# A list-ordered attention and feed-forward kernel: other attention blocks, weights decoded in place, a gate kept in PSUM

## The chip, the cores and the metric

The kernel runs on one core of one Trainium2 chip. The metric is device time in microseconds, the median of the runs, lower is better. Before the change three runs took 772.35, 773.11 and 777.2 us.

## What is computed

Three layers on 4 sequences of 576 positions with 512 channels. q and k are drawn six times wider than v; the weights reach the kernel as float64.

```python
# 1. attention, 8 heads of 64; two results are added
q_d, k_d, v_d = means over 4 neighbouring positions      # 144 positions
out_d = softmax(q_d k_d^T / 8) v_d, each row repeated 4 times
out_local = softmax over |i - j| < 4 of (q k^T / 8), times v
x = out_d + out_local                                    # (4, 576, 512)
# 2. gated feed-forward, 512 -> 1024 -> 512
h = relu(x @ w_in)
c = conv_w[0]*h[s-1] + conv_w[1]*h[s] + conv_w[2]*h[s+1] # per channel
x = (h * sigmoid(c)) @ w_out
# 3. mixer: U is 576 x 32, V is 32 x 576, inner width 2048
u = x + (x^T @ U @ V)^T
out = u + relu(u @ w_ch1) @ w_ch2
```

## The kernel before

**Order.** Tiles come from pools, but no scheduler orders them: a string of some 2,600 words is read word by word, and each word emits a few instructions. So the order on each engine (PE the matrix engine, DVE the vector engine, ACT the scalar engine, POOL, and SP, which issues all DMAs) is the order of the list, and an instruction whose input is not ready holds all behind it on its engine.

**Attention** goes by 16 pairs of heads. q and k land as rows of positions (L315) and are transposed on PE, twelve transposes of 96 columns a pair (`transposes`, L408), then copied out of PSUM (`emit_qc`, `emit_kc`) and summed by fours (`emit_qsum` L439, `emit_ksum` L470). The band of the local part is cut into 10 blocks of 58 queries against 64 keys: a mask product of 320 columns per head (L511), then 20 small float32 products of 64 columns (L517), each with 64 rows of contraction; the trace has two records for each float32 product. The maximum is taken per block and head (L524); exp is one ACT instruction for each block and head, with its row sum as a by-product (L531, ten a pair); `emit_norm` multiplies by reciprocals. P is transposed in five pieces (L599), and 20 products of 58 columns make the local output (L635). The pooled part has three products of 144 columns (L553), six transposes (L604) and four products (L646). For the first eight pairs v is summed by fours on PE, as 20 products with a band matrix (`emit_Vp`, L492); for the other eight on POOL (L480). `emit_x` adds the two outputs in pieces, and `prep_x` splits x into a high and a low part with the columns next to the block's edge.

**Weights.** 16 tiles of 128x512 for layer 2 and 32 for layer 3 arrive as float64, 512 KB each. `decode` turns one into float32 in four steps, one on ACT (L217) and three on DVE (L219, L221, L224); `split_hi` (L229) and `split_lo` (L233) make the two parts.

**The products.** A product of two split operands is three passes. Tokens go in 6 blocks of 384. Layer 2 has 48 units (block and 128 inner channels): `g1` is 12 products of 386 columns (L882), `g2` is 9 of 512 (L944). Between them `relu1` (L893) copies from PSUM to SBUF, `conv_first` (ACT, L912), `conv_rest` (two on DVE, L918), `tanh` (ACT, L922), `gate` (DVE, L927), `gate_hi` (ACT, L932) and `gate_lo` (L935; 20 on POOL, 28 on DVE) follow, all in SBUF, so that the product's bank is free after `relu1`. Layer 3 has 96 units: `g3` (L1051) and `g4` (L1070), with `relu3` between. The mixer's rank-32 products stand between the layers.

**Space.** PSUM has eight banks. During attention four go to attention (`ps0`) and four to layer 2: three sums and one `g`. Before the layer-2 products start, the second four hold q and k transposes.

Of the kernel before, what the change touches and what calls it, by code (L numbers as in the profile page):

```python
# [169 lines left out]
def mixer_kernel(ctx, tc, q, k, v, w_in, conv_w, w_out, mU, mV, w_ch1, w_ch2, out, stop=9, dbg=None, early_end=False):  # L170

    nc = tc.nc
    B, H, S, D = q.shape
    P = 128
# [973 lines left out]
```

## Time and profile before

| | |
|---|---|
| runs | 772.35, 773.11, 777.2 us |
| span of the profiled execution | 771.8 us, 0.2% under the median; the page gives no other time for it |
| PE busy | 750.2 us, 97% |
| DVE busy | 427.6 us, 55%, nearly all in the first 430 us |
| ACT busy | 339.4 us, 44% |
| POOL busy | 158.2 us, 20% |
| moved by DMA | 48.7 MB in 81,203 packets, 61,916 of them under 512 B |

Busy time is the union of an engine's instructions. The matrix engine's records overlap, so that the distance from one start to the next, not the length of one record, is what an instruction costs there.

### The profile page before, as it was taken

The numbers are of one execution on the slowest core, as the hardware profiler recorded it, in microseconds if no ns is written. First come the engines' busy times: TensorE is split into PE (matmuls) and PEld (weight loads), VectorE is DVE, ScalarE is ACT, GpSimd is POOL, SyncE is SP. The second block draws the span as 40 slices with busy tenths as digits, with TensorE's granted clock in tenths as the row PEclk, the third lists the DMA queues.
The fourth block names the chain that finished last, engine by engine and source line by source line (L and its number), as shares of the span: only waits on it lengthen the run. The fifth ranks groups of instructions, "written<-read, shape, count | busy, mean of one in ns | idle before, by whom it ended". The sixth has DMA issues, their size and how long they took to land.

```text
span 771.8 us, 13685 instructions
## 1 busy us (share of the span) xinstructions
PE 750.2 (97%) x5382; PEld 669.8 (87%) x5382; DVE 427.6 (55%) x843; ACT 339.4 (44%) x1025; POOL 158.2 (20%) x233
## 2 busy tenths in 40 slices
PE   4889999999999999999999999999999999999998
PEld 3678888898888998888989889999999899989996
DVE  7888988988897888887888312212121221122111
ACT  3888878777676677675344112111111211111110
POOL 4355257343353111117510000000000000000000
PEclk9999999999999999999999999999999999999999
DMA  9867545343233111211244100100010000001001
GB/s 193 191 158 162 115 123 89 80 79 83 85 103 90 55 55 55 82 55 55 82 137 137 41 1 1 42 1 0 1 42 1 0 26 17 1 1 41 1 1 41
DMA packets 81203, 48.71 MB, mean 63 GB/s; under 512 B 61916, under 2 KB 74484, under 8 KB 81140
## 3 DMA queue, kind: packets, MB, share of 16 engines
q1 hardware_dynamic: 81140, 47.85, 24.0%
q8 instruction: 42, 0.69, 0.4%
q14 instruction: 21, 0.17, 0.1%
HBM read 43.11 MB, written 4.72 MB: 62 GB/s over the span
## 4 chain that ended last, share of the span: by engine, by line
PE 88%; DVE 4%; ACT 3%; DMA 2%; issue 1%; SPq 1%; POOL 0%; DVEq 0%; POOLq 0%; ACTq 0%
PE acc L1070 26%; PE g L1051 13%; PE gb L1051 13%; PE acc L944 11%; PE g L882 10%; PE O L635 3%; PE gb L882 2%; PE tr L408 1%; PE Sd L553 1%; PE O L646 1%; DMA w1t<-in_moe_w_in_dram 1%; PE vp L492 1%; PE S L517 1%; PE T L599 1%; DVE hc L918 1%
## 5 line engine op out<-in xcount | busy, mean ns | idle before, releaser
L1070 PE MATMUL acc<-w,a 128*128 128x512 f32 x864 | 216.5, 394 | 0.1
L1070 PEld LDWEIGHTS acc<-w,a 128*128 128x128 f32 x864 | 160.9, 188 | 29.9 <-ACT a L1059 0.4
L1051 PE MATMUL gb<-uT,w 128*128 128x384 f32 x576 | 111.8, 338 | 0.0
L1051 PE MATMUL g<-uT,w 128*128 128x384 f32 x576 | 111.7, 339 | 0.0
L944 PE MATMUL acc<-w,ghl 128*128 128x512 f32 x432 | 111.5, 396 | 0.1
L1051 PEld LDWEIGHTS gb<-uT,w 128*128 128x128 f32 x576 | 101.7, 188 | 3.8
L1051 PEld LDWEIGHTS g<-uT,w 128*128 128x128 f32 x576 | 101.6, 188 | 3.6
L1060 DVE SCALAR_TENSOR_TENSOR a<-gb,a 128x384 fp32r<-128x384 f32 x48 | 26.7, 557 | 125.1 <-ACT a L1059 125.1
L1060 DVE SCALAR_TENSOR_TENSOR a<-g,a 128x384 fp32r<-128x384 f32 x48 | 26.7, 557 | 123.5 <-ACT a L1059 123.4
L882 PE MATMUL g<-xhl,w 128*128 128x386 f32 (+1 forms) x456 | 93.0, 344 | 0.0
L944 PEld LDWEIGHTS acc<-w,ghl 128*128 128x128 f32 x432 | 79.6, 188 | 14.2 <-POOL ghl L935 0.5
L1059 ACT ACTIVATE a<-g 128x384 fp32r<-128x384 f32 x48 | 23.5, 490 | 141.8 <-PE g L1051 139.7
L882 PEld LDWEIGHTS g<-xhl,w 128*128 128x128 f32 x456 | 80.3, 189 | 4.1 <-issue 0.6
L1059 ACT ACTIVATE a<-gb 128x384 fp32r<-128x384 f32 x48 | 23.5, 489 | 125.1 <-PE gb L1051 119.9
L918 DVE SCALAR_TENSOR_TENSOR hc<-hc,cw 128x384 f32<-128x384 f32 x96 | 64.2, 673 | 9.7 <-ACT hc L912 7.7
L531 ACT ACTIVATE P<-S,nm 122x64 f32<-122x64 f32 x160 | 48.2, 319 | 7.0 <-DVE nm L524 6.0
L935 POOL TENSOR_TENSOR ghl<-hc,ghl 128x384 fp32r<-128x384 f32 x20 | 23.1, 1154 | 84.5 <-ACT ghl L932 84.4
L922 ACT ACTIVATE hc<-hc 128x384 f32<-128x384 f32 x48 | 25.1, 524 | 22.5 <-DVE hc L918 22.5
L531 ACT ACTIVATION_READ_ACCUMULATOR P<-S,nm 122x1 f32 x160 | 33.9, 212 | 0.0
L1039 DVE TENSOR_TENSOR uT<-ut,uT 128x384 fp32r<-128x384 f32 x24 | 13.3, 556 | 32.3 <-ACT uT L1038 32.1
L912 ACT ACTIVATE hc<-hc,cw 128x384 f32<-128x384 f32 x48 | 29.6, 617 | 1.0
L927 DVE SCALAR_TENSOR_TENSOR hc<-hc 128x384 f32<-128x384 f32 x48 | 28.3, 598 | 2.9 <-ACT hc L922 2.6
(139 smaller groups left out, 1016.8 us busy)
## 6 DMA issues: line engine op xcount, KB each, us to landing
wraw<-in_moe_w_ch_dram SPq DMA_DIRECT2D x29, 512.0 KB, 3.6
kr<-in_k_dram SPq DMA_DIRECT2D x32, 144.0 KB, 4.3
qr<-in_q_dram SPq DMA_DIRECT2D x32, 144.0 KB, 4.9
out_dram<-u SPq DMA_DIRECT2D x17, 256.0 KB, 2.1
w1t<-in_moe_w_in_dram SPq DMA_DIRECT2D x8, 512.0 KB, 4.4
w1t<-in_moe_w_out_dram SPq DMA_DIRECT2D x8, 512.0 KB, 4.8
vw<-in_v_dram SPq DMA_DIRECT2D x32, 128.0 KB, 3.8
vr<-in_v_dram SPq DMA_DIRECT2D x8, 288.0 KB
```

The source lines that it names most:

```text
L531: nc.scalar.activation(out=e["P"][:, i, h], in_=e["S", h][:122, i], func=AF.Exp, bias=e["nm"][:, h, i:i + 1], accum_out=e["sm"][:, i, h:h ...
L635: nc.tensor.matmul(O[rows, c:c + QB], e["vw"][rows, 2 * i + a], PT[rows, i, 64 * a:64 * a + QB], start=True, stop=True)
L882: nc.tensor.matmul(p[:, :wd], w[:, a, cc], xhl[g, cc][:, b, :wd], start=k == 0, stop=k == 3 * NCC - 1)
L912: nc.scalar.activation(out=flat(g, c), in_=inner(g, hts[n], 0), func=AF.Copy, scale=cw[:, f:f + 1])
L918: nc.vector.scalar_tensor_tensor(out=o, in0=inner(g, hts[n], k), scalar=cw[:, k * NF + f:k * NF + f + 1], in1=o, op0=ALU.mult, op1=ALU.add)
L922: nc.scalar.activation(out=cts[n], in_=cts[n], func=AF.Tanh)
L927: nc.vector.scalar_tensor_tensor(out=o, in0=o, scalar=1.0, in1=inner(g, hts.pop(n), 1), op0=ALU.add, op1=ALU.mult)
L944: nc.tensor.matmul(acc[g][c], t[:, a, c * P:(c + 1) * P], w[:, b], start=f == 0 and i == 0, stop=f == NF - 1 and i == 2)
L1051: nc.tensor.matmul(p[:, :TB], w[:, a, cc], uT[g, cc][:, b, :TB], start=k == 0, stop=k == 3 * NCC - 1)
L1059: nc.scalar.activation(out=t[:, 0], in_=p[:, :TB], func=AF.Relu)
L1060: nc.vector.scalar_tensor_tensor(out=t[:, 1], in0=p[:, :TB], scalar=0.0, in1=t[:, 0].bitcast(F32), op0=ALU.max, op1=ALU.subtract)
L1070: nc.tensor.matmul(acc2[g][c], t[:, a, c * P:(c + 1) * P], w[:, b], start=f == 0 and i == 0, stop=f == NF2 - 1 and i == 2)
```

## The change

All of the kernel around the two large layers is written anew, and the list with it (2,671 words).

The host lays data out anew, ahead of the timed program: q and k with channels on partitions, v cut into 32-row windows (each row stored more than once) and into groups of four, weights, U and V in the order of their tiles, the identity and the mask as data.

Attention has 24 blocks of 24 queries against 32 keys: per pair two mask products of 192 columns, 48 score products of 32 columns (64 rows of contraction, 24 result rows), softmax by one max, one subtract, one exp and one sum over all 12 groups of a row, three transposes of 128 columns, and 48 products of 24 columns (32 rows of contraction, 64 result rows). q and k are not transposed on PE any more, and v is summed by fours on POOL or DVE for all pairs. PSUM has two slots for attention work while layer 2 runs (`a0`, two banks; `b0`, one), and two banks `g` instead of one.

The convolution, tanh and gate of layer 2 write into the product's own PSUM bank; the gate moves the result to SBUF. All 48 `gate_lo` are on POOL. The raw float64 words land in the tile's final place, are decoded into one of three passing buffers, and the high part is written over the raw words. Three products of zeros (`sp`) stand at the start.

The list's counts up to the first layer-2 product: six pairs scored, four finished, 12.9 MB of loads issued (9 of qk, 576 KB each; 6 of vr, 288 KB; 7 of vw, 384 KB; 6 weights). The same up to the last decode of a weight: all of layer 2 and 15 units of layer 3, as before.

```diff
-        r = p0.tile([96, 6, 2, D], F32, name=f"{nm}r", tag=f"{nm}r", bufs=2)
-        for h in range(2):
-            nc.sync.dma_start(r[:, :, h], src[b, 2 * cc + h].rearrange("(c p) d -> p c d", p=96))
+        t = (xu if p % 3 == 2 else pa).tile([P, 2, S], F32, name="qk", tag=("qk0", "qk1", "xu3")[p % 3])
+        nc.sync.dma_start(t, qk[p])
...
+    def scores(p, n):
+        s = e["S"] = slot_a(n, "S")
+        for h in range(2):
+            nc.tensor.matmul(s[:, h, :6 * NW], identR, mask.rearrange("p j x -> p (j x)"), start=True, stop=False)
+        for k in range(6):
+            t, jh = divmod(k, 2)
+            for a in range(4):
+                i = 4 * (3 * jh + t) + a
+                for h in range(2):
+                    rows = slice(D * h, D * h + D)
+                    nc.tensor.matmul(s[32 * a:32 * a + NQ, h, NW * k:NW * k + NW],
+                                     e["qk"][rows, 0, NQ * i:NQ * i + NQ], e["qk"][rows, 1, WS[i]:WS[i] + NW],
+                                     start=False, stop=k == 5)
...
-        for i in range(5) if part is None else (part,):
-            nc.scalar.activation(out=e["P"][:, i, h], in_=e["S", h][:122, i], func=AF.Exp,
-                                 bias=e["nm"][:, h, i:i + 1], accum_out=e["sm"][:, i, h:h + 1])
+    def shifted(p):       # one subtract of the maxima, S -> P, 384 columns
+        nc.vector.tensor_tensor(...)
+    def exps(p):
+        nc.scalar.activation(out=t, in_=t, func=AF.Exp, scale=SCALE)
+    def rowsums(p):
+        nc.vector.tensor_reduce(out=e["sm"][:, :12], in_=..., op=ALU.add, axis=AX.X)
...
+    def pv_local(p, n):
+        for t in range(3):
+            for a in range(4):
+                for s in range(4):
+                    h, jh = divmod(s, 2)
+                    c = NQ * (4 * t + a)
+                    nc.tensor.matmul(o[D * h:D * h + D, jh, c:c + NQ], e["vw"][32 * s:32 * s + 32, t, a],
+                                     e["PT"][32 * s:32 * s + 32, t, 32 * a:32 * a + NQ], start=True, stop=True)
...
     def conv_first(n):
-        c = cts[n] = hc.pop(n)[:, 1, :TB]
+        c = cts[n] = gp.pop(n)[:, :TB]
...
+    def gate(n, move):
+        if move:
+            cts[n] = ph.tile([P, TB], F32, name="ct", tag="ct", bufs=2)
...
     def gtile():
-        gt[0] += 1
-        if "psb" in pools and gt[0] % 2:
-            return pools["psb"].tile([P, 512], F32, name="gb", tag="gb")
-        return pools["psg"].tile([P, 512], F32, name="g", tag="g")
+        return pools["psg"].tile([P, 512], F32, name="g", tag="g", bufs=2)
```

## Rows read from the trace of the kernel before

**Rows 1.** The page: busy time by engine, and the chain that ended last.

```profile
PE 750.2 (97%) x5382; PEld 669.8 (87%) x5382; DVE 427.6 (55%) x843; ACT 339.4 (44%) x1025; POOL 158.2 (20%) x233
PE 88%; DVE 4%; ACT 3%; DMA 2%; issue 1%; SPq 1%; POOL 0%; DVEq 0%; POOLq 0%; ACTq 0%
```

**Rows 2.** Windows: start and end, length, then each engine's busy time, clock, DMA share, GB/s.

```profile
0.00:20.00 20.00, 9.25 (x78) 7.85 (x79) 14.24 (x29) 8.39 (x27) 9.48 (x38) 1.00 0.98 194
20.00:80.00 60.00, 53.06 (x852) 45.44 (x850) 51.40 (x118) 50.96 (x225) 27.42 (x40) 0.97 0.74 164
80.00:200.00 120.00, 119.93 (x1310) 106.87 (x1310) 105.28 (x238) 93.54 (x348) 54.12 (x79) 1.00 0.43 95
...
380.00:400.00 20.00, 20.00 (x108) 18.21 (x107) 16.80 (x28) 9.54 (x19) 2.57 (x2) 1.00 0.49 148
430.00:772.00 342.00, 338.04 (x1714) 305.04 (x1712) 63.63 (x114) 46.64 (x95) 0.00 (x0) 1.00 0.04 14
```

**Rows 3.** The chain from 60 to 90 us: start, length, engine, tile, line.

```profile
64.20 0.91 PE Sd L553 x6
65.10 0.65 PE O L646 x8
65.75 1.31 PE O L635 x40
...
67.46 1.10 PE g L882 x6
...
70.27 0.32 PE T L599 x3
...
73.55 0.52 PE S L511 x2
74.07 0.72 PE S L517 x40
74.78 1.45 PE vp L492 x40
...
85.77 0.65 PE tr L408 x6
```

**Rows 4.** PE's timeline from 560 us: start, length of the run of records.

```profile
562.35 2.27 PE L1051 MATMUL gb<-uT,w 128*128 128x384 f32 x12
564.46 2.27 PE L1070 MATMUL acc<-w,a 128*128 128x512 f32 x9
566.56 2.27 PE L1051 MATMUL g<-uT,w 128*128 128x384 f32 x12
```

**Rows 5.** DVE's groups by line: busy us, mean ns, idle before.

```profile
L918 DVE SCALAR_TENSOR_TENSOR hc<-hc,cw 128x384 f32<-128x384 f32 x96 | 64.2, 673 | 9.7 <-ACT hc L912 7.7
...
L1060 DVE SCALAR_TENSOR_TENSOR a<-g,a 128x384 fp32r<-128x384 f32 x48 | 26.7, 557 | 123.5 <-ACT a L1059 123.4
...
L935 DVE TENSOR_TENSOR ghl<-hc,ghl 128x384 fp32r<-128x384 f32 x28 | 18.0, 644 | 5.2 <-ACT ghl L932 5.0
L524 DVE TENSOR_REDUCE nm<-S 122x5 f32<-122x320 f32 x32 | 14.9, 481 | 5.1 <-PE S L517 4.8
...
L221 DVE SCALAR_TENSOR_TENSOR wval<-wraw,wval 128x512 uint32<-128x512 uint32 x16 | 12.8, 798 | 0.5
...
L563 DVE TENSOR_REDUCE nmd<-Sd 96x3 f32<-96x432 f32 x16 | 9.5, 595 | 2.1 <-PE Sd L553 2.0
```

**Rows 6.** ACT's groups by line, the same columns.

```profile
L531 ACT ACTIVATE P<-S,nm 122x64 f32<-122x64 f32 x160 | 48.2, 319 | 7.0 <-DVE nm L524 6.0 <-PE vp L492 0.9
L531 ACT ACTIVATION_READ_ACCUMULATOR P<-S,nm 122x1 f32 x160 | 33.9, 212 | 0.0
L912 ACT ACTIVATE hc<-hc,cw 128x384 f32<-128x384 f32 x48 | 29.6, 617 | 1.0
L922 ACT ACTIVATE hc<-hc 128x384 f32<-128x384 f32 x48 | 25.1, 524 | 22.5 <-DVE hc L918 22.5
...
L893 ACT ACTIVATE hc<-g 128x386 f32<-128x386 f32 (+1 forms) x38 | 18.8, 494 | 9.6 <-PE g L882 7.1 <-DVE ghl L935 2.3
```

More of the change, by code (lines that the diff above doesn't have):

```diff
@@ L198, in mixer_kernel @@
[L198 to L213 removed]
+    xu = ctx.enter_context(tc.tile_pool(name="xu", bufs=1, reuse_waits="tile"))
@@ new lines, in clear, with spin_fill, spin, slot_a @@
+    def clear():
+        nc.gpsimd.memset(eps, 1e-9)
+        for t in qds:
+            nc.gpsimd.memset(t, 0.0)
+    def spin_fill():
+        t = pools["spin"] = xu.tile([P, 512], F32, name="spin", tag="xu0")
+        nc.vector.memset(t, 0.0)
+    def spin(n):
+        t = pools["spin"]
+        nc.tensor.matmul(slot_b(n, "spin"), t[:, :P], t, start=True, stop=True)
+    st = {}
+    for p in range(NPAIR):
+        st[p] = {}
+    def slot_a(n, name):
+        return (ps0 if n < 1 else pst).tile([P, 2, 512], F32, name=name, tag=f"a{n}")
@@ new lines, in stats, with view, maxima @@
+    def stats(e):
+        if "sm" not in e:
+            e["nm"] = pa.tile([P, 15], F32, name="nm", tag="nm", bufs=3)
+            e["sm"] = pa.tile([P, 15], F32, name="sm", tag="sm", bufs=3)
+    def view(s):
+        return s[:, :, :6 * NW].rearrange("p h (j x) -> p h j x", j=6)
+    def maxima(p):
+        e = st[p]
+        stats(e)
+        nc.vector.tensor_reduce(out=e["nm"][:, :12].rearrange("p (h j) -> p h j", h=2), in_=view(e["S"]),
+                                op=ALU.max, axis=AX.X, negate=True)
@@ new lines, in scores_d, with maxima_d, exps_d @@
+    def scores_d(p, n):
+        e = st[p]
+        t = slot_b(n, "Sd")
+        s = e["Sd"] = t[:96, :3 * SD].rearrange("p (j x) -> p j x", j=3)
+        for j in range(3):
+            nc.tensor.matmul(s[:, j], e["qd"][:, j], e["ss"][:, 1], start=True, stop=True)
+    def maxima_d(p):
+        e = st[p]
+        stats(e)
+        nc.vector.tensor_reduce(out=e["nm"][:96, 12:], in_=e["Sd"], op=ALU.max, axis=AX.X, negate=True)
+    def exps_d(p):
+        e = st[p]
+        t = e["Pd"] = pa.tile([96, 3, SD], F32, name="Pd", tag="Pd", bufs=2)
+        s = e.pop("Sd")
+        for j in range(3):
+            nc.scalar.activation(out=t[:, j], in_=s[:, j], func=AF.Exp,
+                                 bias=e["nm"][:96, 12 + j:13 + j], accum_out=e["sm"][:96, 12 + j:13 + j])
@@ new lines, in pv_pooled, with copy_od @@
+    def pv_pooled(p):
+        e = st[p]
+        pt = e["PTd"].rearrange("p c (j r) -> p c j r", j=3)
+        for h in range(2):
+            for c in range(2):
+                nc.tensor.matmul(e["O"][D * h:D * h + D, 0, 288:288 + SD].rearrange("p (j r) -> p j r", j=3),
+                                 e["vd"][:, h, c], pt[:, c, :, 48 * h:48 * h + 48], start=c == 0, stop=c == 1)
+    def copy_od(p, eng):
+        e = st[p]
+        t = e["xd"] = pa.tile([P, SD], F32, name="xd", tag="xd", bufs=2)
+        src = e["O"][:, 0, 288:288 + SD]
+        if eng == "ACT":
+            nc.scalar.activation(out=t, in_=src, func=AF.Copy, scale=0.25)
+        else:
+            nc.vector.tensor_scalar(out=t, in0=src, scalar1=0.25, scalar2=None, op0=ALU.mult)
@@ L350, in mixer_kernel @@
-    W1, W2 = {}, {}
-    N1, N2 = 2 * NF, 2 * NF2
-    raws, vals, steps = {}, {}, {}
-    def w_decode(k, make):
-        if k not in steps:
-            vals[k] = make()
-            steps[k] = decode(vals[k], raws[k])
-        next(steps[k], None)
-    pairs = iter(CFG.get("TR", ""))
-    def whole_tile(p, nm):
-        e = st.setdefault(p, {})
-        if nm + "t" not in e:
-            n = next(pairs, "")
-            e[nm + "t"] = pst.tile([P, 2, 512], F32, name="tr", tag="tr" + n, bufs=1 if n else 2)
-        return e[nm + "t"]
@@ L389, in spin @@
-    def spin(bank):
-        nc.tensor.matmul(bank[:, :5 * W], identR, mask, start=True, stop=True)
-    def transposes(p, nm, half=None):
-        if not 0 <= p < NPAIR:
-            return
-        e = st[p]
-        if half is None:
-            t = whole_tile(p, nm)
-            view = [t[:, a, :288] for a in range(2)]
-            e[nm + "ps"] = [(slice(0, S), t[:, :, :288])]
-        else:
-            t = bank([P, 512], "tr")
-            view = {half: t[:, :288]}
-            e[nm + "ps"] = [(slice(288 * half, 288 * half + 288), t[:, :288])]
-        for c in range(6):
-            if half is None or c // 3 == half:
-                nc.tensor.transpose(view[c // 3][:, (c % 3) * 96:(c % 3 + 1) * 96],
-                                    e[nm + "r"][:, c].rearrange("p h d -> p (h d)"), ident[:96, :96])
@@ L619, in half_tile @@
-    def half_tile(e, i):
-        e.setdefault("O", {})
-        if i not in e["O"]:
-            e["O"][i] = bank([P, 512], "O")
-        return e["O"][i]
-    def emit_PV(p, half):
-        if not 0 <= p < NPAIR:
-            return
-        e = st[p]
-        O = half_tile(e, half)
-        for i in (range(0, 4), range(4, 5))[half]:
-            for a in range(2):
-                c = 2 * QB * (i % 4) + QB * a
-                for h in range(2):
-                    rows = slice(64 * h, 64 * h + 64)
-                    nc.tensor.matmul(O[rows, c:c + QB], e["vw"][rows, 2 * i + a], PT[rows, i, 64 * a:64 * a + QB],
-                                     start=True, stop=True)
@@ new lines, in w_dec, with w_hi, w_lo @@
+    def w_dec(*k):
+        *k, step = k
+        k = tuple(k)
+        if step == 0:
+            vals[k] = pv.tile([P, 512], F32, name="wval", tag="wval")
+        dec(raws[k], vals[k], step)
+    def w_hi(*k):
+        pool, tag = w_home(k)
+        W[k] = pool.tile([P, 2, 512], F32R, name="w", tag=tag)
+        nc.scalar.activation(out=W[k][:, 0], in_=vals[k], func=AF.Copy)
+    def w_lo(eng, *k):
+        eng.tensor_tensor(W[k][:, 1], vals.pop(k), W[k][:, 0].bitcast(F32), op=ALU.subtract)
@@ L779, in conv_weights @@
-    def conv_weights():
-        for _ in decode(cval, craw):
-            pass
-        cps = bank([P, 512], "cps")
-        nc.tensor.transpose(cps[:, :NK * NF], cval, ident[:NK * NF, :NK * NF])
-        nc.vector.tensor_copy(cw, cps[:, :NK * NF])
-    pools = {}
-    def open_products():
-        pst.release()
-        pools["psg"] = ctx.enter_context(tc.tile_pool(name="psg", bufs=1, space=PSUM, side="right", reuse_waits="tile"))
-    NSA, NSB = CFG["NSA"], CFG["NSB"]
-    RANK = mU.shape[1]
@@ new lines, in px_hi, with px_lo, g1 @@
+    def px_hi(g, cc):
+        t = xhl[g, cc] = xt.tile([P, 2, XW], F32R, name="xhl", tag="xt")
+        nc.scalar.activation(out=t[:, 0, :runs(g)[1]], in_=px_src(g, cc), func=AF.Copy)
+    def px_lo(g, cc, eng):
+        wd = runs(g)[1]
+        t = xhl[g, cc]
+        eng.tensor_tensor(t[:, 1, :wd], px_src(g, cc), t[:, 0, :wd].bitcast(F32), op=ALU.subtract)
+    hts, cts, ghl, acc, U_, hps, Ht, gp, x2 = {}, {}, {}, {}, {}, {}, {}, {}, {}
+    def g1(n, cc):
+        g, f = divmod(n, NF)
+        wd = runs(g)[1]
+        if cc == 0:
+            gp[n] = gtile()
+        w = W[1, 2 * f].rearrange("p a (c j) -> p a c j", c=NCC)
+        for i, (a, b) in enumerate(((0, 0), (0, 1), (1, 0))):
+            nc.tensor.matmul(gp[n][:, :wd], w[:, a, cc], xhl[g, cc][:, b, :wd],
+                             start=cc == 0 and i == 0, stop=cc == NCC - 1 and i == 2)
@@ L987, in mix_out, with mix_h @@
+    def mix_h(b, part):
+        lo = slice(RANK, 2 * RANK)
+        if part == 0:
+            Ht[b] = pools["pm"].tile([P, DM], F32R, name="Ht", tag="Ht", bufs=2)
+            nc.scalar.activation(out=Ht[b], in_=hps[b], func=AF.Copy)
+        else:
+            nc.vector.tensor_tensor(Ht[b][lo], hps[b][lo], Ht[b][lo].bitcast(F32), op=ALU.subtract)
+    mx = {}
     def mix_out(pair, j):
-        p = pools["psb"].tile([P, DM], F32, name="mx", tag="mx", bufs=2)
+        p = mx[pair, j] = pools["psb"].tile([P, DM], F32, name="mx", tag="mx", bufs=2)
@@ L1056, in relu3, with ut_hi, ut_lo, g3 @@
-    def relu3(m):
-        p = gp.pop(("3", m))
+    def ut_hi(g, cc):
+        t = uT[g, cc] = xt.tile([P, 2, XW], F32R, name="uT", tag="xt")
+        nc.scalar.activation(out=t[:, 0, :TB], in_=ut[g, cc][:, :TB], func=AF.Copy)
+    def ut_lo(g, cc):
+        t = uT[g, cc]
+        nc.vector.tensor_tensor(t[:, 1, :TB], ut.pop((g, cc))[:, :TB], t[:, 0, :TB].bitcast(F32), op=ALU.subtract)
+    def g3(m, cc):
+        g, f = divmod(m, NF2)
+        if cc == 0:
+            gp["3", m] = gtile()
+        w = W[2, 2 * f].rearrange("p a (c j) -> p a c j", c=NCC)
+        for i, (a, b) in enumerate(((0, 0), (0, 1), (1, 0))):
+            nc.tensor.matmul(gp["3", m][:, :TB], w[:, a, cc], uT[g, cc][:, b, :TB],
+                             start=cc == 0 and i == 0, stop=cc == NCC - 1 and i == 2)
```

966 lines of the change are left out of this document (325 added, 641 removed), and 303 rows, old and new, of the table SEQ.

## The prediction

> **What bounds the kernel now.** I read the page's busy line and its chain first: PE is busy 97% of the span and makes 88% of the chain that ended last [rows 1]. So only what shortens PE's own work, or the time in which PE waits, can move the end. Where it waits is read from the windows [rows 2]: 10.75 us in the first 20, 6.94 in the next 60, nearly nothing from 80 to 430, and 3.96 behind 430, mostly the last block's way out; 21.7 us in all. DVE is the second engine to watch: 71%, 86% and 88% busy in the first three windows, and 366 of its 427.6 us lie ahead of 430 us [rows 1, 2]. ACT reaches 85% only from 20 to 80 us. DMA is nearly full in the first 20 us (share 0.98 at 194 GB/s); the weights' later loads moved 148 GB/s at a share of 0.49, so wider rows cost less per byte [rows 2]. Then I read prices from the chain, where each piece is what it put on the path [rows 3], and the pace of the large products [rows 4]: 12 records of 384 columns every 2.11 us and 9 of 512 every 2.10 us, 4.21 us a unit. 144 units make 606 us. None of them is changed: same records, same columns. The change acts on the other 165 us.
>
> **PE work that goes.** Per pair of heads: two sets of q and k transposes, 2 x 0.65 us; two of five P transposes, 2 x 0.107 (three took 0.32); the mask's columns fall from 640 to 384, so 0.52 becomes 0.31 if it goes by columns and stays 0.52 if by records; I take columns, since 320 columns are nearer to the product records than to the small ones [rows 3]. Together 1.72 us, times 16 = 27.5. The band products leave eight pairs, 8 x 1.45 = 11.6 [rows 3]. Removed: 39.1 us. Pooled scores, their transposes and products stay, piece for piece.
>
> **The small products** are the open price. Scores and local output are 20 float32 products each, 40 records, 0.72 + 1.31 = 2.03 us a pair; they become 48 each, 192 records. No row has a product of 32 or 24 columns. Records come every 18 ns for scores and 33 ns for outputs [rows 3]. The scores walk over four places of the array (two heads by two row halves), the outputs over two, and 4 x 18 and 2 x 33 are about the same: one place takes some 66 to 72 ns for 58 to 64 columns. If only that counted, the new scores (half the columns, eight places) would come every 4.5 ns and the new outputs (24 columns, four places) every 6.8, 1.1 us a pair. At the score row's 18 ns per record it is 3.5 us, at the output row's 33 ns it is 6.3. I take 10.5 ns, 2.0 us, as before: the nearest row is the score row, whose places are doubled and columns halved here, but part of its 18 ns may be a floor. So this term is 0, with ends of -15 and +69 us over 16 pairs before anything absorbs it.
>
> A rule speaks against this edit. The Trainium skill, "TensorEngine Tiling (Array Packing)", section Instruction Overhead, says that a matmul costs about 60 cycles however few its columns are and that one should not tile along a side that is already small. By that figure, 25 ns at 2.4 GHz, the two groups would be 4.8 us a pair, 44 us more over the kernel. The score row's 18 ns is already under it, so I don't take it as a floor; the mechanism is a rival below, priced from rows.
>
> **Start.** The first layer-2 product came at 67.5 us [rows 3]. In the new list six pairs are scored and four finished before it. DVE's share: six sums over 1152 columns at 1.35 us (480 ns for 320 columns and 595 for 432 give 1.03 ns a column), six times max, subtract and sum over 384 (0.55 each) and the pooled max (0.60), ten reciprocals at about 0.2, four adds of 576 columns (0.75), eight decode steps (about 0.7) [rows 5], 34 us with small ones. Loads issued ahead are 12.9 MB: 43 us at the later rate (148/0.49 = 302 GB/s), 65 us at today's early rate (194/0.98 = 198) [rows 2]; not all of them are needed by then, and the rows are now 3 to 4.6 KB. So DVE sets it: first data at about 6 us, 34 us of work with gaps, first product at 46 us (40 to 55). PE has done 27 us of work by then: 19 us idle, in the place of 17.7.
>
> **DVE next.** After the start the list is dense in DVE work. Up to the eighth pair's scores DVE has 131 us (the 34 above, then 97 of the same prices, with decode at 2.0 a tile, 0.67 for each low part on DVE, and 1.7 for each gate chain), PE 118. From 80 to 200 us DVE was 88% busy while PE, not DVE, was the limit [rows 2]; as the limit itself I take 94%. 6 + 131/0.94 = 145 us, so PE has 27 us idle by then instead of 19. At 88% it would be 37, at 100% 19. From there on PE has more work than DVE (84 against 57 us, then 87 against 72, 73 against 68), and PE is full again.
>
> **Gate in PSUM.** The two convolution steps cost 673 ns in SBUF; a like instruction with a PSUM operand costs 557 [rows 5], so DVE loses up to 11 us; ACT's 617 and 524 ns may become its 494 from PSUM [rows 6]. I cost this at nothing on the path beyond the DVE sums above. What it adds is a wait: the bank is held from `relu1` to the gate, 0.49 + 0.60 + 2 x 0.56 + 0.52 + 0.56 = 3.3 us in six steps between two engines, about 4 to 5 with crossings. Two banks g and a unit of 4.2 us leave PE, by the list, 3.8 to 8 us of other work until it needs the bank again, in many units about 5. I put 3 us on that (0 to 15): it is hidden except in the tightest units, and behind the waiting PE everything waits.
>
> **The rest.** ACT loses 82 us of exps and accumulator reads for some 9 us of single exps (16 of an estimated 0.55) [rows 6]: worth nothing on the path, as PE covers ACT; without that cover it is the same sign. `gate_lo` wholly on POOL takes 18 us off DVE [rows 5]; 28 more on POOL, even at 2 us each, leave its 158 us [rows 1] far under the span. Decode keeps its four steps. The three starting products lie in a wait for data. SP issues fewer, larger transfers; an early one that waits for a buffer holds those behind it, which I keep in the 40 to 55 above. The end is unchanged, 4 us idle.
>
> **The sum.** 771.8 span - 39.1 PE work + idle of (27 + 3 + 4) - 21.7 = 12.3 gives 745.0. The profiled execution shows only its span, 1.3 us below the median of the runs; with that, **746 us**.
>
> **Rivals.** *Record pitch.* If a small record costs what it cost in the output row, 33 ns, attention grows by (6.3 - 2.0) x 16 = 69 us; the eleven early pairs lie where PE waits for DVE, which absorbs up to 27: 746 + 42 = 788, slower. It decides from about 28 ns, where 4.4 us a pair would be lost to 3.4. For it: more records on smaller work. Against: the score row has 18. Chance 0.09. At 18 ns the same sum gives 746 + 23, less what is absorbed, 757 to 769: 0.11, half of it within 1%.
>
> *The bank wait.* If each of the six steps queues behind a decode step or an attention step of 0.6 to 0.8 us, the chain is 7 to 8 us and PE loses 1 to 2 us in some 40 units: 786 to 826. Against: the list interleaves the units, and most gaps exceed 5. Chance 0.06 for that; a mild form (8 to 15 us more, 754 to 761), with DVE at 88% or a start at 55 beside it, 0.22.
>
> *It comes out better:* 4 to 7 ns per record, a start at 40, DVE full, 705 to 727: 0.10. That the diff doesn't do what it says can hardly be: the transposes are gone from the program. My forecast's own case, 728 to 753, keeps 0.42.
>
> **Chances.** A measurement tells about 1% from no change, so faster is under 765.4. Faster: 0.42 + 0.10 + 0.22 + half of 0.11 = 0.80. Same: the other half and some of the bank wait and pitch rivals' lower ends, 0.10. Slower: 0.10. The range 720 to 770 leaves out the heavy rivals (0.15 or a little less) and the lowest few per cent.
>
> **What would show it.** Right: no transposes of q and k, score and output groups at 10 to 12 ns a record start to start; first layer-2 product near 46 us; PE idle some 27 us ahead of 150 us, DVE over 90% busy there; the large products at 4.2 us a unit. Wrong: PE idle before `g1` put down to the gate; score groups of 1.7 us or more; PE waiting for loads in the first 60 us.

## The result, and the profile after

The changed kernel takes 764.25 us (median of 4 runs, 763.52 to 765.76); the ratio to the kernel before is 0.9874, 95% interval 0.9839 to 0.9909. It is faster, by 9 us instead of the 27 forecast: direction and range held, the size did not. The profiled execution has a span of 762.7 us, 1.5 us under the median.

The page: busy time by engine, and the chain that ended last.

```profile
PE 736.5 (97%) x6634; PEld 652.8 (86%) x6634; DVE 397.6 (52%) x661; ACT 298.7 (39%) x682; POOL 172.3 (23%) x161
PE 83%; DVE 11%; issue 2%; ACT 1%; DMA 1%; SPq 0%; POOL 0%; DVEq 0%; POOLq 0%; ACTq 0%
```

Against [rows 1] PE's busy time fell by 13.7 us, not by the 39.1 of work removed: 25.4 us came back as busy time. PE's idle time is 762.7 - 736.5 = 26.2 us, 7.8 less than the 34 forecast. The two make up the miss in the span: 25.4 - 7.8 = 17.6 of 762.7 - 745.0 = 17.7 us. So the step to look for made PE's work dearer; it did not add to PE's waits.

The windows, with the columns of [rows 2]; the third column from the right is the granted clock.

```profile
0.00:20.00 20.00, 12.09 (x348) 8.27 (x349) 12.59 (x26) 9.72 (x30) 8.91 (x17) 0.99 0.92 317
20.00:40.00 20.00, 19.00 (x503) 16.38 (x502) 10.58 (x19) 9.17 (x30) 7.60 (x9) 0.58 0.78 236
40.00:60.00 20.00, 17.92 (x357) 15.69 (x358) 15.12 (x25) 12.25 (x39) 10.71 (x11) 0.66 0.61 196
60.00:80.00 20.00, 16.36 (x357) 14.19 (x356) 19.22 (x29) 14.29 (x37) 12.66 (x11) 0.91 0.51 168
80.00:100.00 20.00, 16.72 (x345) 14.15 (x347) 19.16 (x33) 15.85 (x42) 10.71 (x11) 0.91 0.76 255
...
260.00:320.00 60.00, 58.67 (x287) 51.30 (x285) 52.63 (x80) 41.97 (x82) 27.21 (x22) 1.00 0.09 29
...
430.00:762.00 332.00, 328.95 (x1668) 296.48 (x1666) 60.64 (x108) 44.99 (x92) 0.00 (x0) 1.00 0.03 13
```

The kernel before, in two of the same stretches:

```profile
20.00:40.00 20.00, 15.82 (x227) 12.94 (x226) 17.68 (x38) 17.33 (x78) 6.52 (x9) 0.91 0.78 185
40.00:60.00 20.00, 17.80 (x328) 15.00 (x331) 17.01 (x41) 16.59 (x77) 10.01 (x13) 1.00 0.64 148
```

From 20 to 60 us PE is busy 92% of the time, at 0.58 and 0.66 of the full clock, that is mostly at 1.2 of 2.4 GHz. (1 - clock) times length over the first 100 us gives 19.0 us of lost clock time, against 1.8 before. DVE, which the forecast made the limit of the start, is busy 53% from 20 to 40: between 6 and 60 us it waits 6.3 us for PE's scores and 8.9 us for ACT's copies of the pooled outputs, which themselves wait 7.3 us for PE.

The chain of waits from 16 us on: start, length, what was on the path.

```profile
16.41 0.57 PE O L425 x27
16.98 3.11 issue
20.09 2.12 PE O L425 x69
...
46.36 2.70 PE O L425 x96
49.06 1.16 PE O L433 x8
50.23 1.70 PE Sd L364 x6
51.93 0.02 issue
51.95 0.60 DVE nm L369
...
77.71 1.25 DVE wval L484
78.98 1.68 DVE wval L486
80.69 1.21 DVE wval L489
...
90.61 1.52 PE O L425 x96
```

From 16 to 52 us the chain is PE and its stalls, but for one ACT copy of 0.64 us. From 52 to 120 us it runs mostly through DVE: 41 of the 68 us, with 15 on PE (in the kernel before PE has 58 there and DVE nothing). In the middle of one group of local products PE stands 3.11 us in which it waits for nothing that the profile shows ("issue"; the last section says what ends such stalls); the trace of before has no such stall in its first 120 us. Behind it the same 96 records take 2.70 us in place of the 1.52 that they take at full clock (the last row). PE's timeline shows prices at full clock: the distance from one start to the next.

```profile
76.63 0.36 PE L304 MATMUL S<-mask,identR 128*128 128x192 f32 x2
76.92 1.00 PE L311 MATMUL S<-qk 64*24 64x32 f32 x96
77.85 0.81 PE L618 MATMUL g<-xhl,w 128*128 128x386 f32 x3
...
184.70 2.27 PE L618 MATMUL g<-xhl,w 128*128 128x386 f32 x12
186.81 2.25 PE L672 MATMUL acc<-w,ghl 128*128 128x512 f32 x9
188.90 2.81 PE L618 MATMUL g<-xhl,w 128*128 128x386 f32 x15
```

Scores: 0.93 us for 96 records, 9.7 ns each; the mask 0.29; the large products 2.11 + 2.09 = 4.20 us a unit, unchanged. DVE's groups, columns as in [rows 5], and the spread of one of them (min, median, max ns):

```profile
L645 DVE SCALAR_TENSOR_TENSOR g<-h,cw,g 128x384 f32<-128x384 f32 x96 | 59.3, 619 | 27.6 <-ACT g L640 26.0
L486 DVE SCALAR_TENSOR_TENSOR wval<-raw,wval 128x512 uint32<-128x512 uint32 x48 | 43.1, 898 | 1.3
L489 DVE SCALAR_TENSOR_TENSOR wval<-raw,wval 128x512 uint32<-128x512 uint32 x48 | 42.5, 889 | 1.1
L656 DVE SCALAR_TENSOR_TENSOR ct<-g,h 128x384 f32<-128x384 f32 x48 | 26.4, 550 | 6.8 <-POOL ghl L664 3.4 <-ACT g L649 3.3
```

```profile
L489 DVE SCALAR_TENSOR_TENSOR wval<-raw,wval x48: 678/692/1675, 42.9 to 410.0; 128x512 uint32<-128x512 uint32 x48
```

The convolution step fell from 673 to 619 ns in PSUM. A decode step (L486 or L489) is 0.69 us in the median, but 0.89 in the mean, with some above 1.6.

### The profile page after: what moved, and what is told of

Read it like the earlier page. It is cut to its first block, busy times and chain, and to the rows that moved or that the text cites. A ratio compares the mean times of both kernels' runs of the same rounds, so it can differ in the third digit from the quotient of the medians.

```text
span 762.7 us, 15404 instructions
## 1 busy us (share of the span) xinstructions
PE 736.5 (97%) x6634; PEld 652.8 (86%) x6634; DVE 397.6 (52%) x661; ACT 298.7 (39%) x682; POOL 172.3 (23%) x161
## 4 chain that ended last, share of the span: by engine, by line
PE 83%; DVE 11%; issue 2%; ACT 1%; DMA 1%; SPq 0%; POOL 0%; DVEq 0%; POOLq 0%; ACTq 0%
PE g L746 25%; PE acc L764 25%; PE g L618 10%; PE acc L672 10%; PE O L425 3%; DVE wval L486 2%; DVE wval L489 2%; PE Sd L364 2%; PE S L311 2%; PE O L433 1%; DVE g L645 1%; DVE wval L484 1%; PE Td L405 1%; DVE ss L287 1%; PE h L696 1%
## 5 line engine op out<-in xcount | busy, mean ns | idle before, releaser
L746 PE MATMUL g<-uT,w 128*128 128x384 f32 x1152 | 214.2, 338 | 0.9 <-DVE a L755 0.9
L746 PEld LDWEIGHTS g<-uT,w 128*128 128x128 f32 x1152 | 202.3, 188 | 7.2 <-DVE a L755 2.7
L672 PEld LDWEIGHTS acc<-w,ghl 128*128 128x128 f32 x432 | 79.7, 188 | 17.2 <-POOL ghl L664 0.9
L664 POOL TENSOR_TENSOR ghl<-ct,ghl 128x384 fp32r<-128x384 f32 x48 | 53.0, 1105 | 94.7 <-ACT ghl L661 89.1
L645 DVE SCALAR_TENSOR_TENSOR g<-h,cw,g 128x384 f32<-128x384 f32 x96 | 59.3, 619 | 27.6 <-ACT g L640 26.0
L505 POOL TENSOR_TENSOR w<-wval,w 128x512 fp32r<-128x512 f32 x31 | 42.7, 1379 | 77.5 <-ACT w L502 73.2
L502 ACT ACTIVATE w<-wval 128x512 fp32r<-128x512 f32 x48 | 30.1, 630 | 40.5 <-DVE wval L489 40.2
L486 DVE SCALAR_TENSOR_TENSOR wval<-raw,wval 128x512 uint32<-128x512 uint32 x48 | 43.1, 898 | 1.3
L489 DVE SCALAR_TENSOR_TENSOR wval<-raw,wval 128x512 uint32<-128x512 uint32 x48 | 42.5, 889 | 1.1
L425 PEld LDWEIGHTS O<-PT,vw 32*64 32x64 f32 x1536 | 27.5, 148 | 7.8 <-issue 5.7
L425 PE MATMUL O<-PT,vw 32*64 32x24 f32 x1536 | 29.4, 223 | 4.0 <-issue 3.1
L482 ACT ACTIVATE wval<-raw 128x512 f32<-128x512 f32 x48 | 31.1, 663 | 1.5 <-DVE w L505 1.0
```

Source lines behind the costliest of these rows:

```text
L425: nc.tensor.matmul(o[D * h:D * h + D, jh, c:c + NQ], e["vw"][32 * s:32 * s + 32, t, a], e["PT"][32 * s:32 * s + 32, t, 32 * a:32 * a + NQ] ...
L486: nc.vector.scalar_tensor_tensor(out=d, in0=lo, scalar=29, in1=d, op0=ALU.logical_shift_right, op1=ALU.bitwise_or)
L489: nc.vector.scalar_tensor_tensor(out=d, in0=hi, scalar=0x80000000, in1=d, op0=ALU.bitwise_and, op1=ALU.bitwise_or)
L505: eng.tensor_tensor(W[k][:, 1], vals.pop(k), W[k][:, 0].bitcast(F32), op=ALU.subtract)
L645: nc.vector.scalar_tensor_tensor(out=o, in0=inner(g, hts[n], k), scalar=cw[:, k * NF + f:k * NF + f + 1], in1=o, op0=ALU.mult, op1=ALU.add)
L664: eng.tensor_tensor(ghl[n][:, 1], cts.pop(n), ghl[n][:, 0].bitcast(F32), op=ALU.subtract)
```

## The experiments

All times against the kernel before, which ran beside each. "First relu" is when ACT starts the first unit's `relu1`; "clock lost" is (1 - granted clock) times length over the first 120 us; "stall" is PE's idle time there that the profile calls issue.

| kernel | us | ratio, 95% interval | first relu | clock lost | stall |
|---|---|---|---|---|---|
| before | 773.1 | 1 | 70.5 | 1.8 | 0 |
| after | 764.25 | 0.9874 (0.9839 to 0.9909) | 61.7 | 19.0 | 3.1 |
| e1_dense | 774.18 | 1.0015 (0.9997 to 1.0033) | 68.9 | 15.6 | 4.3 |
| e2_loads | 765.97 | 0.9898 (0.9871 to 0.9926) | 60.7 | 22.2 | 2.2 |
| e3_both | 773.52 | 0.9989 (0.9971 to 1.0008) | 68.2 | 15.6 | 3.4 |
| e4_nosign | 756.28 | 0.9784 (0.9744 to 0.9824) | 64.7 | 20.8 | 6.2 |
| e5_two | 766.19 | 0.9911 (0.9881 to 0.9941) | 62.6 | 15.6 | 6.9 |
| e6_noscore | 754.54 | 0.9757 (0.9729 to 0.9784) | 56.4 | 25.2 | 0 |
| e7_gateact | 762.57 | 0.9855 (0.9831 to 0.9878) | 62.9 | 20.6 | 5.2 |
| e9_evact | 766.30 | 0.9903 (0.9871 to 0.9934) | 61.9 | 20.6 | 6.3 |
| e10_pool | 768.61 | 0.9930 (0.9908 to 0.9952) | 60.9 | 19.0 | 3.4 |
| e11_early | 768.02 | 0.9937 (0.9918 to 0.9955) | 64.7 | 20.6 | 4.2 |
| e12_both | 768.93 | 0.9950 (0.9931 to 0.9969) | 64.7 | 15.6 | 5.9 |
| e13_twonoscore | 754.41 | 0.9752 (0.9721 to 0.9783) | 56.1 | 22.2 | 0 |
| e14_fill | 764.88 | 0.9886 (0.9851 to 0.9922) | 64.4 | 17.4 | 6.8 |
| e15_spin0 | 768.20 | 0.9928 (0.9902 to 0.9954) | 62.8 | 17.2 | 5.2 |
| e16_noscoresign | 742.93 | 0.9603 (0.9574 to 0.9632) | 56.7 | 22.2 | 0 |
| e17_nolow | 757.40 | 0.9795 (0.9765 to 0.9825) | 59.7 | 15.6 | 4.6 |
| e18_pvlate | 791.62 | 1.0248 (1.0194 to 1.0301) | 63.1 | 17.4 | 6.1 |
| e19_pvearly | 788.33 | 1.0207 (1.0181 to 1.0234) | 81.8 | 29.0 | 12.7 |

### Does the clock alone make the loss? e1, e2, e3, e5, e13, e14, e15

First, dense products of zeros on the path, and weight loads moved back; e3 joins both.

```diff
+    def dense(t, p):                       # e1, e3: pairs 0 to 5, ahead of S, T, Td and V
+        if p < 6:
+            w = pools["spin"]
+            nc.tensor.matmul(t[:, :256], w[:, :P], w[:, :256], start=True, stop=True)
-  "... lw.1 sp.1 lw.2 wl.1.0 lc wl.1.1 qs.0 wl.1.2 ... lq.5 ..."
+  "... sp.1 qs.0 ... lq.5 lw.1 lw.2 wl.1.0 lc wl.1.1 wl.1.2 ..."    # e2, e3
```

> For the first six pairs one float32 product of 256 columns on the whole array (zeros) stands ahead of each group of scores, P transposes, pooled transposes and local outputs, in the same PSUM bank; it is overwritten. Theory 'clock': the 18 us that the forecast missed are mostly PE at half clock (0.58 and 0.66 granted from 20 to 60 us in the changed kernel), and it stays there because small products fill the array thinly. Then the granted clock from 20 to 54 us rises to 0.85 or more, the first layer-2 product comes at 45 to 48 us instead of 51.5, and the time is 752 to 758 us although 24 products were added. Rival 'gaps': the clock follows PE's idle gaps alone, or DVE sets the start: clock as before, the added products cost 5 to 15 us where PE is the limit, 766 to 778 us.

> Two v loads, the first three weight loads and the convolution's weights are issued behind the sixth qk load instead of ahead of the fourth (order on SP alone). Theory 'fetch': the 3.1 us in which PE stood at 17 us with nothing that the profile shows to wait for is a fetch of its own instructions behind full DMA queues (share 1.05), and it is what let the clock fall at 20 us. Then the stall falls under 1.5 us, the clock stays full to 35 us or longer, and the time is 754 to 760. Rival: the fetch is late by itself, since small products use up instructions quickly: a stall of 2 to 4 us stays, clock 0.5 to 0.7 from 20 to 40 us, time 762 to 767.

> Both edits together. Theories 'clock' and 'fetch' both right: 748 to 755 us, granted clock over 0.9 from 20 to 60 us, first layer-2 product at 42 to 46 us. If only one works, its own time; if neither, 766 to 778.

e1 and e3 granted more clock (0.74 to 0.83 from 20 to 60 us, under the 0.85 and 0.9 asked for), but the 24 added products cost more than that gave: the first relu came 7 us later, and the times are the rivals'. e2 lost the stall at 17 us, and the clock fell all the same; another stall of 2.2 us came at 40. No gain in any. Then cheaper attempts: two products once, on the path (e5; e13 in the kernel without scores), or in a wait (e15; e14 with the weight loads later).

```diff
         s = e["T"] = slot_b(n, "T")
+        for _ in range(2 if p == 1 else 0):          # e5, e13; p == 0 in e14, e15
+            nc.tensor.matmul(s, pools["spin"][:, :P], pools["spin"], start=True, stop=True)
-  "... wl.1.0 lc wl.1.1 qs.0 wl.1.2 ... lq.4 ..."
+  "... qs.0 ... lq.4 wl.1.0 lc wl.1.1 wl.1.2 ..."    # e14
```

> Two float32 products of 512 columns of zeros stand once ahead of the P transposes of the second pair; nothing else differs from the changed kernel (764.2 us). They cost PE 2 to 5 us at 22 to 27 us of the span, where it runs at half clock. Theory 'clock' (the start is late because small products at half clock do not bring the full clock back): the clock is full from about 27 to 40 us, the two score and output groups there take 1.0 and 1.5 us in place of 1.5 and 2.7, and the time is 759 to 763. Rival (each fall follows a wait that stays, so that the clock falls again and the two products are only work): 764 to 769, first layer-2 product at 52 us or later.

> The kernel without score products (754.5 us; its attention weights are wrong) with the two products of zeros of 512 columns ahead of the second pair's P transposes. That kernel had no stall in which PE waited for nothing the profile shows, and half clock in much of the first 80 us. Theory 'half clock costs, and the instruction feed took back what the two products gave before': no such stall over 1 us appears, granted clock over 0.75 from 20 to 60, and 749 to 752. Rival (the clock gives nothing whatever the feed does): 753.5 to 757.

> Two products of zeros of 512 columns stand ahead of the P transposes of the first pair, in the 1.9 us (12.2 to 14.1) in which PE waits for POOL's normalised P; they cost the path nothing. Theory 'half clock follows the idle time' : with that gap filled the clock stays full beyond 20 us although the 3 us stall at 17 us stays; half-clock time in the first 60 us falls from 31 to under 20, and the time is 757 to 762. Rival (the stall alone starts the fall, or a start at full clock waits for DVE, POOL and instructions instead): 763 to 766.

> As the kernel before, and the first three weight loads and the small load among them are issued behind the fifth pair's q and k. Theory 'half clock and the instruction stall are the start's loss': no stall over 1 us in which PE waits for nothing shown ahead of 35 us, clock full to 35 us, first relu of layer 2 at 55 to 59, time 753 to 759. Rival (the start is then set by DVE and POOL, or the stall comes later): first relu at 60 or later, 762 to 767.

None of the four gained: e5, e13 and e14 came out in the rival's range, e15 above it (768.20, where the rival had 763 to 766). The timeline of e5:

```profile
22.07 2.12 PE L427 MATMUL O<-PT,vw 32*64 32x24 f32 x69 [4.24 <-issue]
24.12 3.78 PE L397 MATMUL T<-spin 128*128 128x512 f32 x4
```

The clock from 20 to 40 rose to 0.83, but the two products took 3.6 us, the stalls grew from 3.1 to 6.9, and from 60 to 80 the clock was lower than in the changed kernel (0.69 to 0.91). In e15 the fall moved, too:

```profile
20.00:40.00 20.00, 17.30 (x461) 15.02 (x464) 10.67 (x21) 8.80 (x29) 6.83 (x9) 0.57 0.83 236
40.00:60.00 20.00, 14.40 (x413) 11.73 (x407) 18.26 (x27) 12.98 (x41) 10.98 (x13) 0.97 0.69 213
```

At 0.97 PE idles 5.6 us of 20 there, partly in a new stall of 1.56. The expectation that the gap before 14 us starts the fall failed: with it filled, the clock still fell. e13 has no stall and more clock from 20 to 40 than e6 (0.76 to 0.59), and gains nothing over it either. What the table adds: no edit brought the lost clock time under 15.6 us. They moved it, so they do not show what the start would take at full clock; that was not reached. Nor does lost clock time by itself sort the kernels: e6 and e13 lose more of it than the changed kernel (25.2 and 22.2 us) and are 10 us faster.

### What do the small products cost? e6, e19, e18

e6 leaves the 48 score products of a pair out; e19 and e18 issue the 48 local output products twice, for the first six and the last five pairs.

```diff
-        for k in range(6):                 # e6: no score products, the mask closes the group
...
-                                     start=False, stop=k == 5)
+        for _ in range(2 if p < 6 else 1):     # e19; p > 10 in e18
+            for t in range(3):
...
```

> The 48 small score products of each pair are left out (96 records, 0.94 to 1.5 us a pair; the mask alone makes the scores, so the attention weights are wrong); all else stays. PE loses 16 to 19 us of work in all. Theory 'record price counts in full' (PE is the limit wherever attention stands): 745 to 749. Theory 'PE waits for DVE ahead of 150 us' (so that most early groups are covered, and only the five late pairs count): 757 to 761. If the clock falls for longer because PE has still less to do: 761 to 766.

> The same for the first six pairs, ahead of 60 us. PE has 9.1 us more work at full clock, 16.5 at half. Theory 'the small products set the start' (with the half clock and the instruction feed): first relu of layer 2 at 71 or later and 773 to 781. Rival (DVE sets the start): first relu at 62 to 66 and 764 to 768.

> The 48 local output products of the last five pairs are issued twice (the result is the same). By the price in the timeline, 1.52 us for 96 records at full clock, PE has 7.6 us more work behind 200 us, where it is full: 771 to 773. Rival (records overlap with other products' weight loads, or the lists' waits absorb them): under 769.

e6 gained 9.7 us of 15.0 (16 x 0.94): between the two theories, 5.3 of it already at the first relu, and its stalls are gone. The other third did not reach the end. It is not shown what took it: e6 also loses 6.2 us more clock time, and its PE waits more for ACT and POOL (in the first 120 us 5.7 us for ACT's scaled sums of q, 2.5 before the edit). e19 fits "the small products set the start" and goes past it: 9.1 us of work at full clock made the time 24.1 us longer, the first relu 20.1 later. e18 fits neither theory: 27.4 us for 7.6 of work, where PE is full and nothing else changed. Its timeline and windows:

```profile
176.78 2.51 PE L426 MATMUL O<-PT,vw 32*64 32x24 f32 x155
180.59 0.77 PE L426 MATMUL O<-PT,vw 32*64 32x24 f32 x37 [1.31 <-issue]
181.29 1.09 PE L434 MATMUL O<-PTd,vd 72*64 72x144 f32 x8
...
260.06 1.05 PE L426 MATMUL O<-PT,vw 32*64 32x24 f32 x27 [2.64 <-issue]
261.04 1.24 PE L434 MATMUL O<-PTd,vd 72*64 72x144 f32 x8
262.21 4.21 PE L673 MATMUL acc<-w,ghl 128*128 128x512 f32 x9
266.21 0.79 PE L398 MATMUL T<-ident,P 128*128 128x128 f32 x3
```

```profile
150.00:200.00 50.00, 48.69 (x607) 43.69 (x607) 29.12 (x49) 24.86 (x58) 18.21 (x17) 0.97 0.12 35
200.00:260.00 60.00, 55.88 (x1056) 49.60 (x1055) 31.53 (x62) 27.26 (x75) 14.35 (x15) 0.89 0.13 44
260.00:320.00 60.00, 58.52 (x478) 51.49 (x478) 44.47 (x65) 37.05 (x74) 22.67 (x19) 0.91 0.08 27
```

155 records go at 16 ns, then PE stands for nothing shown, then the clock is half, and nine large records take 4.0 us (262.21 to 266.21) in place of 2.1. Half clock begins within 1 us of the end of each of five such stalls, two of them of 0.71 us. The sum comes near: 7.6 of work, 6.2 of stalls (1.31 + 0.71 + 0.82 + 2.64 + 0.71), and (0.03 x 50 + 0.11 x 60 + 0.09 x 60) = 13.5 of lost clock time, 27.3 against 27.4. That it closes to 0.1 us is luck, as the four times of e18 span 8.5 us and its first relu, ahead of the edit, is 1.4 us later. In the changed kernel groups of 96 between large products, at the same place, show no stall and clock 1.00.

### Is DVE a limit? e4, e17, e7, e9, e10, e11, e12, e16

e4 leaves the fourth decode step out, e17 the third. e7 makes the gate's second part an ACT copy.

```diff
-  "... wd.1.0.3 ... wd.2.31.3 ..."      # e4: the 48 words of step 3 go; e17: those of step 2
-        eng.tensor_tensor(ghl[n][:, 1], cts.pop(n), ghl[n][:, 0].bitcast(F32), op=ALU.subtract)
+        nc.scalar.activation(out=ghl[n][:, 1], in_=cts.pop(n), func=AF.Copy)      # e7
```

> Leaves out the fourth decode step (the sign) of all 48 weight tiles: 48 x 0.89 = 43 us of DVE less, nothing else moved; weights become absolute values. Theory 'DVE': where DVE is 96% busy (54 to 120 us, 260 to 300, 320 to 380) it is the limit, PE's idle there (8.4 + 3 us) goes, and the half-clock stretches after 60 us with it: 750 to 757 us. Theory 'clock' alone: only the start matters, where two to four such steps lie: 761 to 764 us.

> The third decode step (which puts the last three of a weight's 24 bits in place, a relative 2 to the power of -21) is left out for the weights of both layers; the rest is computed as in the changed kernel. Theory 'DVE is late in layer 2' (the kernel without the fourth step took 756.3): 755 to 758, first relu of layer 3's unit 20 5 us or more ahead. Rival (that gain was of that run's order): 762 to 766.

> The second part of the gate's output is a plain copy on ACT in place of POOL's subtraction of two operands (48 instructions of 1.1 us leave POOL, 48 of about 0.5 us come to ACT; the low part is therefore wrong, the products on it stay). Theory 'port' (POOL's subtractions slow DVE's decode steps, 0.89 us here against 0.69 to 0.9 before): the means of the two middle decode steps fall to 0.75 or less, DVE loses 10 us or more of busy time, and the time is 757 to 761. Rival (the decode step's price is its own): the two means stay within 0.03 us of 0.89, and the time is 763 to 766.

e4 gained 8.0 us, e17 6.9, both in the range of the theory that DVE is a limit. In e17 PE no longer waits late:

```profile
260.00:320.00 60.00, 60.00 (x298) 53.22 (x297) 47.59 (x78) 42.80 (x83) 25.91 (x22) 1.00 0.16 54
320.00:360.00 40.00, 40.00 (x201) 35.58 (x199) 29.94 (x50) 24.77 (x47) 13.93 (x11) 1.00 0.41 143
```

So e17, which keeps 21 of each weight's 24 bits, is the fastest kernel here that has whole attention and signs, ahead of the kernels before and after the change. In e7 the two long decode steps fell to 0.835 and 0.830 us (the first one's row below) and DVE's busy time by 10.7 us. The theory's 0.75 was not reached, the rival's 0.86 to 0.92 neither, and the time (762.57) is not told apart from the changed kernel's.

```profile
L486 DVE SCALAR_TENSOR_TENSOR wval<-raw,wval 128x512 uint32<-128x512 uint32 x48 | 40.1, 835 | 1.3
```

Then four edits of the list that keep all work. e9 gives DVE's PSUM copies to ACT, e10 DVE's late low parts to POOL, e11 puts three tiles' decode into DVE's idle time at 20 us and each later one a tile earlier, e12 is e10 and e11.

```diff
-  "xdv.8 ... ev.0.1 ... cv.10 ... cdv.15"
+  "xd.8 ... ea.0.1 ... c.10 ... cd.15"                                        # e9
-  "mL.0.0 ... wO.2.1"
+  "ml.0.0 ... wo.2.1"                                                         # e10
-  "wd.1.0.2 Sd.2.0 ..."
+  "wd.1.0.2 wd.1.1.0 wd.1.0.3 wd.1.2.0 wd.1.1.1 wd.1.1.2 wh.1.0 ... Sd.2.0 ..."   # e11
```

> All copies out of PSUM that the list gives to DVE (sums of layer 2, P transposes, two pooled outputs; about 20 instructions, some 11 us) go to ACT; what is computed stays the same. Theory 'DVE is the limit ahead of 150 us and again from 240 to 430': DVE's queue is 11 us shorter, about half of it in those stretches, so 759 to 762. Rival (the limit there is the wait for the product's bank, or ACT's own queue): 763 to 767, and PE's waits for the gate or the eviction stay or grow.

> The 14 low parts of layer-3 weights and the 10 low parts of the mixer's input that the list gives to DVE go to POOL; what is computed stays the same. DVE loses some 18 us between 245 and 430 us of the span, POOL gains about 26. Theory 'DVE is the limit late in layer 2' (PE stood 3 us between 260 and 400, each time on DVE): PE is full there and the time is 760 to 762.5. Rival (POOL's subtractions are late, and slow DVE's decode steps beside them): the decode steps' mean rises over 0.9 us and the time is 764 to 769.

> Of the layer-2 weights, the first three tiles' decode stands in DVE's idle time at 20 to 25 us of the span, and each later tile's stands where its forerunner's stood; what is computed and all other order stay the same. Theory 'decode in the wrong place' (DVE idle 14 of the 40 us from 20 to 60, then the limit to 110): first relu of layer 2 at 58 to 60 us in place of 61.7, PE's waits for POOL's low part gone, time 757 to 761. Rival (PE's half clock and its instruction feed set the start, and DVE's sums behind it): first relu at 61 or later, 763 to 766.

> The edits of the two kernels before it together; what is computed stays the same. If both stretches are limited by DVE, the gains add: 753 to 759. If only the early one, 757 to 761; if neither, 763 or more.

None gained. e9, e10 and e12 came out in their rivals' ranges, e11 (768.02) slower than either of its two; e10, e11 and e12 are about 4 us slower than the change. In e10 the steps rose, as its rival said, to means of 0.94 and 0.97 us (the second one's row below). The kernels that leave POOL's work as it was show 0.86 to 0.94, so that the rise is a small one:

```profile
L481 DVE SCALAR_TENSOR_TENSOR wval<-raw,wval 128x512 uint32<-128x512 uint32 x48 | 46.4, 970 | 1.2
```

A low part that cost DVE 0.7 us costs POOL 1.38. In e11 PE waits 5.5 us for POOL's normalised P, 3.6 more than before the edit: the low parts now stand ahead of it in POOL's order. Moving work from DVE to POOL is no relief here; doing less is. Last, the two gains together:

> Score products and the fourth decode step (of both layers' tiles) are left out together; attention weights and weights' signs are therefore wrong. Alone they gave 9.7 and 8.0 us. If the early and the late loss are two separate limits, they add: 745 to 748. If they are one and the same (DVE is late in both), 751 to 755.

e16 is 21.3 us under the change, more than 9.7 + 8.0. So the small products and DVE are two limits, not one, and without both the time is 3 us under the forecast. Why the two together give 3.6 us more than their sum is not shown.

## Why the prediction was wrong

**The work removed** (39.1 us) was priced rightly. The busy time of PE can be divided among its groups by adding, for each record, the distance to the next start, waits left out. So counted, the trace of before has 20.0 us of transposes of q and k and 13.2 us of band products, against 20.8 and 11.6 taken; both are gone. The mask takes 0.29 us at full clock against 0.31 taken.

**The small products** failed, first in size: 9.7 ns per score record and 15.8 per output record (1.52 us for 96), 12.8 on average against the 10.5 taken. That is 2.46 us a pair instead of 2.0, 7.4 us over 16. The term was put at nothing because one pair's rows had 2.03 us for the old products; over all pairs these put 35.1 us on PE, 2.19 a pair, and the new ones 39.7 at their full-clock price, so that the step itself cost 4.7 us. The average lies in the 5.7 to 33 that the bounds spanned. The rival at 18 ns was too dear for the record itself, and its time, 757 to 769, came true by another road, which is luck. The rule of the Trainium skill, "TensorEngine Tiling (Array Packing)", section Instruction Overhead, from which I had worked out 25 ns a matmul, is not borne out by these rows, taken by records as I had worked it out; the score row of before already hinted that.

**The clock and the stall** were not priced at all: the step that failed most. The sum took one price per record wherever it stands. The start, in which six pairs' small products have no large ones between them, came with a stall of 3.1 us and 17.2 us more lost clock time than before (19.0 - 1.8). Set against the full-clock price of the same groups, the records that ran at half clock took 16.5 us more, against 1.5 before: 15.0 us of busy time. The three starting products of zeros, priced at nothing, keep PE busy for 5.1 us; they lie in a wait, so they lengthen nothing and take as much off the idle time. With the 4.7 these make 24.8 of the 25.4 that came back.

That such stalls and the half clock cost time in full is shown where PE is the limit (e18), and that more small products early cost far more than their work is shown by e19. How the loss of the first 52 us reached the end is shown in part: PE makes the chain that far, and DVE, which waited for it, had then done 38.3 us of work by 60 us, where the forecast's 94% from 6 us on would have given 50.8; DVE leads the chain from there to 120 us. That the start would have been so much shorter at full clock is argued, not shown: no kernel reached it. What makes the clock fall is open as well. It is not the score products or the stalls alone, since without both (e6) more clock time was lost.

**The start.** 46 us was forecast for the first layer-2 product, set by DVE; it came at 51.5, set by PE (the chain, e19, e6). The forecast of 19 us of idle before it was 9.0 (51.5 less 42.5 busy). Some 5 of the 10 us between are the products of zeros; for the rest PE was slower, so it waited less.

**DVE next.** My count of the list was off: the eighth pair's scores came at 77 us, and the 131 us of DVE work that I put ahead of them were done, by busy time, only at about 163. The idle time forecast by 145 us was 27; it was 19.4 up to 150. DVE was over 90% busy from 60 to 100 (96%), as the forecast's test asked, not in the 40 us before. How far this moved the sum is not shown. Two figures of the forecast do not come out, and no term uses them: DVE's work ahead of 430 us is 364 us by [rows 2], not 366, and 192 records at 28 ns are 3.4 us over the 2.0, not 4.4.

**Decode** at 0.67 to 0.7 us a step is the median, not the mean: 2.3 us a tile (0.51 + 0.90 + 0.89), not 2.0. "PE is full again" behind 150 us held but for 3 us.

**Gate in PSUM.** The convolution fell from 673 to 619 ns, half the gain allowed. The wait put at 3 us measured 1.3 (the row below); that PE idles 3.0 us between 260 and 400 us in all is chance, the rest being for other DVE work:

```profile
L618 PE MATMUL g<-xhl,w 128*128 128x386 f32 (+1 forms) x229 | 45.1, 341 | 1.3 <-DVE ct L656 1.3
```

That row is of PE's lines from 244.9 to 437.5 us. The bank wait as a rival (786 and more) is ruled out. A kernel with the gate chain back in SBUF was not tried, so what the change gained or lost by it is not shown.

**The tail** (4 us idle) and the large products held.

## What to carry to other kernels

Price a change that trades a few wide products for many narrow ones by the place where they stand: between large products a group of 96 records cost just its records, in a row with others it also cost stalls and half clock, in one run more than three times its work. Where small products open a kernel, look at their number before reordering the other engines: having fewer of them gained 9.7 us (e6), and every edit of order lost or gained nothing. Mixing them with large products that have to be done anyway is what the undisturbed groups behind 120 us suggest; it was not tried. And check a mean against its median before costing 96 steps by either: the spread may be a neighbour engine that a move of work will make worse.

## What the runs showed of the hardware

- PE can stand for microseconds within one run of like instructions with no shown wait: 0 us in the first 120 before, 3.1 after, 12.7 with doubled products, none with the scores left out. The DMA list names an instruction queue whose packets (16 KB each) number 52 after and 40 without the 768 score products, 256 bytes a product. These are PE's own instructions: its matrix and weight-load records divided by 256 make 51.8, 39.8 in e6 and 42.05 before, for 52, 40 and 42 packets. The times of the single packets, which the traces hold beside the views, settle what ends the stalls: of the 56 in all kernels together, 53 end 1.0 to 1.7 us after such a packet has landed, where a moment taken at random from 12 to 100 us, where most stalls lie, does so in 11 of 100 cases. So PE was waiting for its next instructions. A packet holds 128 records with their weight loads, which is 2.0 us of local products at 15.8 ns, while the large products of layer 3 draw one every 25 us. The Trainium skill, "Runtime: NRT & Kernel Launch", section Instruction fetch mechanics, has the cost of the next block mostly hidden. It is so in the kernel before, with no stall; the stall of 2.64 us in e18 speaks against it for such small records: its packet set out 0.5 us after PE had stopped, at a DMA share of 0.08 to 0.13. What makes a packet set out late no run here shows.
- The clock was half behind PE's idle stretches and stayed so while PE was 95% busy with small products (20 to 37 us), and in e18 large products ran at half clock behind such a stall.
- Work on POOL slows decode steps on DVE: 0.89 us in the mean with POOL's subtractions (0.86 to 0.94 over the kernels that leave them alone), 0.83 without the gate's, 0.94 to 0.97 with more of them (e10), 0.69 in the median. The Trainium skill, "SBUF — State Buffer", section SBUF: two separate sides, says that a DVE instruction with two operands in SBUF and a GpSimd one that reads there exclude each other for a whole instruction; these means and the maximum of 1.68 us agree with it; no run here separates the port from other causes.
